# Attention decode with a sliding window: VectorE's and ScalarE's written-out orders become one loop each, and quad 7 gets PSUM banks of its own

## The chip, the cores and the metric

The kernel runs on one core of a Trainium2 chip. The metric is the device time in microseconds (us) of one execution; lower is better. The kernel before took 183.55 us (median of three runs, 183.39 to 183.97).

## The reference

One decoding step of attention with grouped heads over the last W = 512 positions of a cache, with both projections. All data are bf16.

```python
q = (x @ wq).reshape(B, 1, 32, 128).transpose(0, 2, 1, 3)          # B = 32, D = 512
k = repeat(k_cache[:, :, Sk - W:, :], 4, axis=1)                  # 8 heads of keys and values
v = repeat(v_cache[:, :, Sk - W:, :], 4, axis=1)                  # Sk = 2048, Dh = 128
p = softmax(einsum("bhqd,bhkd->bhqk", q, k) * 128 ** -0.5)
out = einsum("bhqk,bhkd->bhqd", p, v).transpose(0, 2, 1, 3).reshape(B, 1, 4096) @ wo
```

The window of the keys is 33.5 MB, that of the values as much, and wq and wo are 4.2 MB each: 75.5 MB are read.

## The kernel before

The 32 sequences are worked on in eight **quads** of four (NQ = 8). A quad q has a load of keys Kq and one of values Vq, 4.2 MB each, and K_sb and V_sb hold two quads each (buffer q % 2). Every step of a quad is an operation with a letter, and every engine has a list of them that is run strictly in order:

- **T**q.w (VectorE, `turn`, L514): the two halves of the keys are turned by 32 x 32 blocks, into KT_sb. It needs Kq, and the scores of the quad before to have read KT_sb.
- **S**q.w (TensorE, `scores`, L340): 16 matmuls for each half give the scores in the PSUM bank S_ps.
- **M** (VectorE): the largest score of a row; **X** (ScalarE): the exponential and its sum; **N** (VectorE): the division, into P_bf.
- **E** (TensorE, `to_value_rows`, L356): 16 matmuls bring the weights to the rows of the values, in EP_ps; **G** (ScalarE) copies them to PTc; **B**q.h (both engines, four heads each) spreads them into bd[q % 2].
- **P**q.a.b (TensorE, `pv`, L368): groups a to b of the 32 groups (four matmuls each) of weights times values, into the four banks O_ps.
- **C**q.r (either engine): a quarter of the rows is picked from O_ps into C_sb; **F** (TensorE, `fold`, L380): eight matmul records that fold it; **D** (ScalarE): the result goes to o_sel.

The orders are text at L19 to L38. TensorE has a head, a loop of three rounds of two quads (L22, L440), and a tail. In a round the quad c is worked on while the values of the quad before it, b, are multiplied; the order is `S{c}.0 S{c}.1 F{a} P{b}.0.12 E{c} P{b}.12.16 P{b}.16.20 P{b}.20.32`, with a the quad before b. For c = 5 this reads S5.0 S5.1 F3 P4.0.12 E5 and the rest of P4. VectorE and ScalarE have a list for all eight quads (L30, L35), without a loop. VectorE's list is not regular: T1.0 stands ahead of M0, T6.0 ahead of M5, T6.1 ahead of N5 and B5, T7.0 ahead of N6 and T7.1 ahead of B6:

```python
T4.1 M4 N4 B4.0.4 T5.0 C3.2.3 T5.1 C3.3.4 T6.0 M5 T6.1 N5 B5.0.4 C4.2.4 M6 T7.0 N6 T7.1 B6.0.4
C5.2.4 M7 N7 B7.0.5 C6.2.4 C7.2.4
```

`needs` (L105) says which operations an operation waits for; one engine's waits for another's are made from it, one semaphore for an engine and a kind of operation.

SyncE issues the large loads in the order of L40: K0 K1 V0 K2 V1 K3 V2 K4 V3 K5 K6 V4 K7 V5 V6 V7 W, where V5, V6 and V7 are two pieces each and W (wo) three. Kq waits for T of quad q - 2, Vq for the P that last read its buffer, and wo, which takes the place of the even keys, for T6.1. The three loads of wo cover rows 0 to 21, 22 to 29 and 30 to 31 of each partition (L46), and the last matmuls (L467) wait for them one after the other.

The eight PSUM banks are S_ps, EP_ps, four for O_ps, F_ps and Y_ps (L180). Since every quad's values go to the same O_ps, Pq waits for all four Cq-1.

Ahead of quad 0, x is turned and multiplied with wq, the eight PSUM banks of queries are copied one at a time (L505, L559), and VectorE turns them (L508).

Of the kernel before, what the change touches and what calls it, by code (L numbers as in the profile page):

```python
# [19 lines left out]
S0.0 S0.1 S1.0 S1.1 E0 E1 P0.0.32  # L20
# [6 lines left out]
P7.0.18 P7.18.32 F6 F7  # L27
"""
ROUNDS = 3
DVE_OPS = """  # L30
T0.0 T0.1 T1.0 M0 T1.1 N0 M1 N1 B0.0.4 B1.0.4 T2.0 T2.1 M2 N2 B2.0.4 T3.0 T3.1 M3 N3 B3.0.4 T4.0
T4.1 M4 N4 B4.0.4 T5.0 C3.2.3 T5.1 C3.3.4 T6.0 M5 T6.1 N5 B5.0.4 C4.2.4 M6 T7.0 N6 T7.1 B6.0.4
C5.2.4 M7 N7 B7.0.5 C6.2.4 C7.2.4
"""
ACT_OPS = """  # L35
X0 X1 G0 B0.4.8 G1 B1.4.8 C0.0.4 X2 D0 G2 B2.4.8 C1.0.4 X3 D1 G3 B3.4.8 C2.0.4 X4 D2 G4 B4.4.8
C3.0.2 X5 D3 G5 B5.4.8 C4.0.2 X6 D4 G6 B6.4.8 C5.0.2 X7 D5 G7 B7.5.8 C6.0.2 C7.0.2 D6 D7
"""  # L38
# [7 lines left out]
WOP = [(0, 22), (22, 30), (30, 32)]  # L46

# [5 lines left out]
def bass_standalone__sliding_block_cached__sampling_kernel(  # L53
# [22 lines left out]
    NG = 4  # L76
# [7 lines left out]
    orders = {"PE": head + sum(rounds, []) + tail, "DVE": ops_of(DVE_OPS), "ACT": ops_of(ACT_OPS)}  # L84

    ends, total = {}, {}
    for eng, ops in orders.items():
        for op in ops:
            kind = op[0]
            key = ("ANY", "C") if kind == "C" else (eng, kind)  # L90
            total[key] = total.get(key, 0) + (op[3] - op[2] if kind == "C" else 1)
            if kind == "C":
                ends["C", op[1]] = key + (4 * op[1] + 4,)
            elif kind == "B":
                for i in range(op[2], op[3]):
                    ends[kind, op[1], i] = key + (total[key],)
            elif kind == "P":
                for g in range(op[2], op[3]):
                    ends["P", op[1], g] = key + (total[key],)
            elif kind == "D":  # L100
                ends[op] = key + (total[key] + 1,)
            else:
                ends[op] = key + (total[key],)

    def needs(op):  # L105
# [3 lines left out]
        if kind == "T":  # L109
            d = [("S", q - 1, op[2])]  # L110
        elif kind == "S":
            d = [("T", q, op[2]), ("X", q - 1)]
        elif kind == "M":
            d = [("S", q, 1)]
        elif kind == "X":
            d = [("M", q), ("N", q - 1)]
        elif kind == "N":
            d = [("X", q), ("E", q - 1)]
        elif kind == "E":
            d = [("N", q), ("G", q - 1)]  # L120
        elif kind == "G":
            d = [("E", q)] + spread(q - NG)
        elif kind == "B":
            d = [("G", q), ("P", q - 2, 31)]
        elif kind == "P":
            d = spread(q) + [("C", q - 1)]
        elif kind == "C":
            d = [("P", q, 31), ("F", q - 2)]
        elif kind == "F":
            d = [("C", q)]  # L130
        elif kind == "D":
            d = [("F", q)]
        return [ends[n] for n in d if n[1] >= 0]

    with ExitStack() as es:
# [3 lines left out]
        K_sb = [sb(f"K_sb{i}", [P, R * DH], BF16) for i in range(2)]  # L139
# [9 lines left out]
        PTc = sb("PTc", [P, NG, R, REP], BF16)  # L149
        C_sb = sb("C_sb", [P, 2, 4, DH], F32)  # L150
        o_sel = sb("o_sel", [P, NI, B], BF16)
# [3 lines left out]
        maxv = sb("maxv", [P, NQ], F32)  # L155
        negmax = sb("negmax", [P, NQ], F32)
        sums = sb("sums", [P, NQ], F32)
        recip = sb("recip", [P, NQ], F32)
# [10 lines left out]
        F_id = spare[:, 1280:1536].bitcast(F32).rearrange("p (r h) -> p r h", r=4)  # L169
        m_id = spare[:, 1536:1792].bitcast(F32).rearrange("p (b h k) -> p b h k", b=4, h=HKV)  # L170
        F_hd = spare[:, 1792:1856].bitcast(F32)
        m_red = spare[:, 1856:1920].bitcast(F32)
# [7 lines left out]
        S_ps, EP_ps, O_ps, F_ps, Y_ps = ps[:, 0], ps[:, 1], ps[:, 2:6], ps[:, 6], ps[:, 7]  # L180

        def folds(q):
            return (F_ps if q < NQ - 1 else S_ps)[:, 0:4 * NI]
# [57 lines left out]
        def _(sp):  # L241
            wait = Waits(sp)
            wo_h = wo.rearrange("(h r) n -> h (r n)", r=DH)
            wo_r = wo_h.rearrange("h (d m) -> h d m", d=4)
            for op in ops_of(" ".join(LOADS)):
                kind, q = op[0], op[1]
                if kind == "K":
                    if q >= 2:
# [13 lines left out]
                else:  # L262
                    wait([ends["T", NQ - 2, 1]])
                    i0, i1 = WOP[q]
                    sp.dma_start(
                        wo_sb[:, i0:i1, :].rearrange("p i n -> p (i n)"),
                        wo_r[:, :, i0 * D:i1 * D],
                    ).then_inc(sem_wo[q], 16)
# [3 lines left out]
        def _(pool):  # L272
# [10 lines left out]
            pool.sem_inc(op_sem["ACT", "D"], 1)  # L283
# [3 lines left out]
            diag(F_id[:, :, :], [[-32, 4], [-1, HQ]], "pool_f")  # L287
            diag(m_id[:, :, :, :], [[-32, 4], [-4, HKV], [-1, KB]], "pool_m")
# [30 lines left out]
        def _(pe):  # L319
# [48 lines left out]
            def pv(q, g0, g1):  # L368
                for g in range(g0, g1):
                    for b in range(4):  # L370
                        pr = slice(32 * b, 32 * b + 32)
                        ins = pe.matmul(  # L372
                            O_ps[:, b, :],
# [6 lines left out]
            def fold(q):  # L380
                for d in range(4):
# [3 lines left out]
                        rhs=C_sb[:, q % 2, :, NI * d:NI * d + NI],  # L385
# [11 lines left out]
            def waits_of(op):  # L397
# [3 lines left out]
                if kind == "S" and op[2] == 0:  # L401
                    yield ("ONE", "pool_qbd"), 4 * (q // 2) + 4
                    if q == 0:
                        yield ("ONE", "dve_q"), 4
                        yield ("ONE", "act_q"), 4
                elif kind == "E" and q == 0:
                    yield ("ONE", "pool_e"), 2
                elif kind == "F" and q < NQ - 1:
# [51 lines left out]
            for j, (i0, i1) in enumerate(WOP):  # L460
                pe.wait_ge(sem_wo[j], 16)
                last = j == len(WOP) - 1
                for cs in ((0, 1), (2, 3)) if last else (range(4),):
                    for i in range(i0, i1):
                        for c in cs:
# [3 lines left out]
                                lhsT=o_sel[:, i, :],  # L469
# [6 lines left out]
        def spread_args(q, h):  # L476
            return bd[:, q % 2, :, h, :], PTc[:, q % NG], mask[:, h:h + 1]

        def pick_args(q, r):
            pr = slice(32 * r, 32 * r + 32)  # L480
            return C_sb[pr, q % 2], O_ps[pr, :, r * DH:(r + 1) * DH]

        @block.vector
        def _(dve):
            wait = Waits(dve)
# [5 lines left out]
            dve.tensor_reduce(  # L491
                F_hd[:, :], F_id[:, :, :].rearrange("p r h -> p h r"), AX.X, ALU.add
            ).then_inc(s["dve_c"], 1)
            dve.wait_ge(s["pool_m"], 2)
            dve.tensor_reduce(
                m_red[:, :].rearrange("p (h k) -> p h k", h=HKV),
                m_id[:, :, :, :].rearrange("p b h k -> p h k b"), AX.X, ALU.add,
            ).then_inc(s["dve_c"], 1)
            dve.wait_ge(s["dve_c"], 2)
            dve.tensor_reduce(  # L500
                mask[:, :], m_red[:, :].rearrange("p (h k) -> p h k", h=HKV), AX.X, ALU.add
            ).then_inc(s["dve_c"], 1)
            for n in range(4):
                dve.wait_ge(s["pe_q"], 2 * n + 1)
                dve.tensor_copy(Q_row[:, 1024 * n:1024 * n + 512], ps[:, 2 * n]).then_inc(s["dve_q"], 1)  # L505
            dve.wait_ge(s["dve_q"], 4)
            dve.wait_ge(s["act_q"], 4)
# [6 lines left out]
            def turn(q, w):  # L514
                dve.wait_ge(sem_k[q % 2], 16 * (q // 2 + 1))
                return dve.transpose(  # L516
                    KT_sb[:, w].bitcast(F32).rearrange("p r c t -> p r (c t)"),
                    K_sb[q % 2][:, :].bitcast(F32).rearrange("p (r w c) -> p r w c", r=R, w=2)[:, :, w],
                )

            def maxes(q):
                dve.tensor_reduce(maxv[:, q:q + 1], S_ps, AX.X, ALU.max).then_inc(s["dve_m"], 1)  # L522
                dve.wait_ge(s["dve_m"], q + 1)
                return dve.tensor_scalar(  # L524
                    negmax[:, q:q + 1], maxv[:, q:q + 1], -SCALE, None, op0=ALU.mult)

            def norm(q):
                dve.reciprocal(recip[:, q:q + 1], sums[:, q:q + 1]).then_inc(s["dve_r"], 1)
                dve.wait_ge(s["dve_r"], q + 1)
                return dve.tensor_scalar(  # L530
                    P_bf[:, :], P_f32[:, :], recip[:, q:q + 1], None, op0=ALU.mult)

            def spread(q, h0, h1):
                for h in range(h0, h1):
                    o, i, m = spread_args(q, h)
                    ins = dve.tensor_scalar(o, i, m, None, op0=ALU.mult)  # L536
                return ins

            def pick(q, r0, r1):
                for r in range(r0, r1):  # L540
                    dve.tensor_copy(*pick_args(q, r)).then_inc(op_sem["ANY", "C"], 1)  # L541

            run = {"T": turn, "M": maxes, "N": norm, "B": spread, "C": pick}
            for op in orders["DVE"]:
                wait(needs(op))
                ins = run[op[0]](*op[1:])
                if ins:
                    ins.then_inc(op_sem["DVE", op[0]], 1)
# [4 lines left out]
        def _(act):  # L553
            wait = Waits(act)
            act.wait_ge(s["pool_j"], 1)
            act.activation(junk[:, 1:2], junk[:, 0:1], ACTF.Exp).then_inc(s["act_warm"], 1)
            for n in range(4):
                act.wait_ge(s["pe_q"], 2 * n + 2)
                act.activation(  # L559
                    Q_row[:, 1024 * n + 512:1024 * n + 1024], ps[:, 2 * n + 1], ACTF.Copy  # L560
                ).then_inc(s["act_q"], 1)
            act.wait_ge(s["dve_c"], 3)

            def exponential(q):
                return act.activation(  # L565
                    P_f32[:, :].rearrange("p (k r) -> p k r", k=KB),
                    S_ps.rearrange("p (r k) -> p k r", k=KB), ACTF.Exp,
                    bias=negmax[:, q:q + 1], scale=SCALE, accum_out=sums[:, q:q + 1],
                )

            def gather(q):
                return act.activation(  # L572
# [57 lines left out]
```

## Time and profile before

| | us |
|---|---|
| median of three runs | 183.55 |
| profiled execution | 183.87 |
| its span (first to last instruction) | 182.6 |
| TensorE matmul busy | 118.9 |
| VectorE busy | 105.8 |
| ScalarE busy | 49.7 |
| mean DMA rate over the span | 415 GB/s |
| mean granted TensorE clock | 0.822 |

In the profile's rows, PE is TensorE (PEld its weight loads), DVE is VectorE, ACT is ScalarE, POOL is GpSimd and SPq is SyncE's queue of DMA issues. A row of the timeline gives its start, its length, the engine, the line of the kernel, the operation, what it writes and reads with the shape, and the count; the bracket gives the idle time of the engine just before it, and what ended that. A row of stages gives for each stretch its length, then each engine's busy time with its count of instructions, then the granted TensorE clock, the share of time in which the DMA engines were busy, and their rate.

### The profile page before, as it was taken

How to read it: one execution, taken by the hardware profiler on the slowest of the kernel's cores; microseconds unless marked ns; L12 is line 12 of the kernel's file. 1: busy time of each engine (PE TensorE's matmuls, PEld its weight loads, DVE VectorE, ACT ScalarE, POOL GpSimd, SP SyncE). 2: the span in 40 equal slices, each digit the busy share in tenths (PEclk: the TensorE clock that was granted, in tenths of full speed). 3: DMA queues.
4: the chain of work that ended last, by engine and by line, in shares of the span. 5: the costliest groups of instructions: out<-in, count | busy, mean ns of one | idle time of the engine just before them, and what ended most of it. 6: DMA issues, size and time to landing. Idle time of an engine off the chain costs nothing.

```text
span 182.6 us, 3659 instructions
## 1 busy us (share of the span) xinstructions
PE 118.9 (65%) x1636; PEld 57.6 (32%) x1636; DVE 105.8 (58%) x101; ACT 49.7 (27%) x92; POOL 12.4 (7%) x34
## 2 busy tenths in 40 slices
PE   0029901425869898049954899334299869996984
PEld 0013300101535353015521453003035434552553
DVE  0031499999559713983279317999902799633030
ACT  3001300000490527402470107100106406443031
POOL 7400012000300000003000000003000000000000
PEclk9999995555769999756995589755559999999999
DMA  6999999999999999999999999999999999999991
GB/s 235 461 431 409 424 459 438 431 395 460 449 431 388 449 456 416 395 452 449 425 398 438 438 447 409 431 438 445 424 416 416 427 424 438 416 436 437 424 374 56
DMA packets 3461, 75.70 MB, mean 415 GB/s; under 512 B 412, under 2 KB 508, under 8 KB 636
## 3 DMA queue, kind: packets, MB, share of 16 engines
q1 hardware_dynamic: 3360, 75.52, 96.7%
q8 instruction: 7, 0.11, 0.3%
q10 hardware_dynamic: 92, 0.05, 0.1%
q14 instruction: 2, 0.02, 0.0%
HBM read 75.53 MB, written 0.03 MB: 414 GB/s over the span
## 4 chain that ended last, share of the span: by engine, by line
DMA 39%; PE 28%; DVE 25%; ACT 3%; issue 3%; SPq 0%; DVEq 0%
DVE KT_sb L516 20%; DMA K_sb<-in_k_cache_dram 16%; DMA V_sb<-in_v_cache_dram 16%; PE ps L372 16%; DMA V_sb<-in_wq_dram 7%; PE ps L334 5%; PE ps L346 3%; DVE QT_sb L508 2%; PE ps L360 2%; ACT bd L578 1%; PE ps L382 1%; DVE C_sb L541 1%; PE ps L467 1%; DVE maxv L522 1%; DVE bd L536 1%
## 5 line engine op out<-in xcount | busy, mean ns | idle before, releaser
L516 DVE STREAM_TRANSPOSE KT_sb<-K_sb 128x4096 f32<-128x4096 f32 x16 | 70.5, 4429 | 4.6 <-DMA K_sb<-in_k_cache_dram 4.5
L372 PE MATMUL ps<-V_sb,bd 32*128 32x512 bf16 x1024 | 62.7, 398 | 9.6 <-DMA V_sb<-in_v_cache_dram 6.5
L346 PE MATMUL ps<-KT_sb,QBD 128*32 128x512 bf16 x256 | 24.6, 527 | 36.2 <-DVE KT_sb L516 32.1
L372 PEld LDWEIGHTS ps<-V_sb,bd 32*128 32x128 bf16 x1024 | 27.0, 97 | 40.5 <-issue 9.8
L346 PEld LDWEIGHTS ps<-KT_sb,QBD 128*32 128x32 bf16 x256 | 6.6, 113 | 52.4 <-DVE KT_sb L516 35.4
L536 DVE TENSOR_SCALAR bd<-PTc,mask 128x512 bf16<-128x512 bf16 x33 | 9.4, 349 | 22.5 <-ACT PTc L572 22.5
L565 ACT ACTIVATE P_f<-ps,negmax 128x512 f32<-128x512 f32 x8 | 5.5, 689 | 58.0 <-DVE negmax L524 58.0
L578 ACT ACTIVATE bd<-PTc,mask 128x512 bf16<-128x512 bf16 x31 | 19.9, 712 | 0.3
L583 ACT ACTIVATE C_sb<-ps 32x512 f32<-32x512 f32 x22 | 13.0, 589 | 21.7 <-PE ps L372 21.4
L541 DVE COPY C_sb<-ps 32x512 f32<-32x512 f32 x10 | 6.9, 693 | 12.9 <-PE ps L372 12.7
L312 POOL COPY QBD<-QT_sb 32x256 bf16<-32x256 bf16 x16 | 6.3, 396 | 106.0 <-PE ps L346 91.2
L572 ACT ACTIVATE PTc<-ps 128x512 bf16<-128x512 f32 x8 | 4.8, 595 | 27.9 <-PE ps L360 27.9
L382 PE MATMUL ps<-C_sb,F_pad 128*128 128x128 f32 x64 | 12.0, 345 | 0.4 <-DVE C_sb L541 0.4
L382 PEld LDWEIGHTS ps<-C_sb,F_pad 128*128 128x128 f32 x64 | 10.2, 242 | 4.8 <-issue 2.9
L360 PE MATMUL ps<-P_bf,E_sb 128*128 128x128 bf16 x128 | 9.5, 233 | 2.2 <-DVE P_bf L530 2.2
L334 PE MATMUL ps<-V_sb,bd 128*128 128x512 bf16 x32 | 9.2, 459 | 1.9 <-DMA V_sb<-in_wq_dram 1.9
L360 PEld LDWEIGHTS ps<-P_bf,E_sb 128*128 128x128 bf16 x128 | 8.1, 105 | 6.3 <-issue 3.4
L522 DVE TENSOR_REDUCE maxv<-ps 128x1 f32<-128x512 f32 x8 | 5.5, 687 | 7.5 <-PE ps L346 7.5
L323 PE MATMUL ps<-bd 32*128 32x128 bf16 x4 | 0.6, 294 | 10.6 <-DMA bd<-in_x_dram 10.6
L487 DVE CAST bd<-ps 128x512 bf16<-128x512 f32 x1 | 0.7, 691 | 11.3 <-PE ps L323 11.3
L559 ACT ACTIVATE KT_sb<-ps 128x512 bf16<-128x512 f32 x4 | 2.4, 598 | 17.1 <-PE ps L334 17.1
L505 DVE CAST KT_sb<-ps 128x512 bf16<-128x512 f32 x4 | 2.8, 692 | 6.7 <-PE ps L334 6.7
(29 smaller groups left out, 31.0 us busy)
## 6 DMA issues: line engine op xcount, KB each, us to landing
K_sb<-in_k_cache_dram SPq DMA_DIRECT2D x8, 4096.0 KB, 24.6
V_sb<-in_v_cache_dram SPq DMA_DIRECT2D x5, 4096.0 KB, 29.4
V_sb<-in_v_cache_dram SPq DMA_DIRECT2D x4, 2048.0 KB, 21.0
V_sb<-in_wq_dram SPq DMA_DIRECT2D x1, 4096.0 KB, 12.3
K_sb<-in_wo_dram SPq DMA_DIRECT2D x1, 2816.0 KB, 20.9
V_sb<-in_v_cache_dram SPq DMA_DIRECT2D x1, 2304.0 KB, 13.1
V_sb<-in_v_cache_dram SPq DMA_DIRECT2D x1, 1792.0 KB, 14.8
K_sb<-in_wo_dram SPq DMA_DIRECT2D x1, 1024.0 KB, 22.7
```

The source lines that it names most:

```text
L312: pool.tensor_copy(QBD[pr].rearrange("p u a (h c) -> p u a h c", h=HKV).rearrange("p u (w t) h c -> p (u w) t h c", w=2)[:, :, :, :, 4 * b ...
L334: ins = pe.matmul(ps[:, n], lhsT=xT_sb[:, kt, :], rhs=wq_sb[:, kt, n * 512:(n + 1) * 512], start=kt == 0, stop=kt == DKT - 1, tile_positio ...
L346: ins = pe.matmul(S_ps[32 * c:32 * c + 32, :], lhsT=QBD[:, q % 2, 2 * w + t, c0:c0 + 32], rhs=KT_sb[:, w, :, KB * h:KB * h + KB, t], start ...
L360: ins = pe.matmul(EP_ps[:, e * R:(e + 1) * R], lhsT=window[:, KB - 1 - k:KB - 1 - k + P], rhs=P_bf[:, k * R:(k + 1) * R], start=k == 0, st ...
L372: ins = pe.matmul(O_ps[:, b, :], lhsT=bd[pr, q % 2, 4 * g:4 * g + 4].rearrange("p r h e -> p (r h e)"), rhs=V_sb[q % 2][pr, 512 * g:512 * ...
L382: ins = pe.matmul(folds(q), lhsT=F_sb[:, d].rearrange("p h d -> p (h d)"), rhs=C_sb[:, q % 2, :, NI * d:NI * d + NI], start=d == 0, stop=d ...
L516: return dve.transpose(KT_sb[:, w].bitcast(F32).rearrange("p r c t -> p r (c t)"), K_sb[q % 2][:, :].bitcast(F32).rearrange("p (r w c) -> ...
L522: dve.tensor_reduce(maxv[:, q:q + 1], S_ps, AX.X, ALU.max).then_inc(s["dve_m"], 1)
L536: ins = dve.tensor_scalar(o, i, m, None, op0=ALU.mult)
L541: dve.tensor_copy(*pick_args(q, r)).then_inc(op_sem["ANY", "C"], 1)
L578: ins = act.activation(o, i, ACTF.Copy, scale=m)
L583: act.activation(*pick_args(q, r), ACTF.Copy).then_inc(op_sem["ANY", "C"], 1)
```

## The change

1. **VectorE and ScalarE run a loop over the eight quads.** Its body is, for quad n, on VectorE: T n.0, T n.1, C of quad n - 2 (its rows 2 and 3), M n, N n, B n (heads 0 to 3). On ScalarE: X n, D of quad n - 2, G n, B n (heads 4 to 7), C of quad n - 1 (rows 0 and 1). What is left of quads 6 and 7 follows the loop. Buffers and semaphore levels are chosen by registers, and the semaphores start from levels that SyncE adds (BIAS), so that the first iterations need no special case. PTc, the maxima and the sums have one buffer in place of four or eight.
2. **Quad 7's values go to PSUM banks 4 to 7**, the other quads' to banks 0 to 3. P7 waits for D5 in place of C6. The folds of quads 6 and 7 go to banks 0 and 1.
3. **The loads of wo** are cut at elements 11264 and 15616 of a partition's 16384, and the last 768 elements (1536 B) come in two loads, of 125 and of 3 partitions.
4. In TensorE's head, E0 stands ahead of S1, and P0 is cut in pieces; P7 is cut in four pieces in place of two. TensorE's loop is unchanged.
5. The copies of the queries are two of 1024 columns on each engine in place of four of 512, and one small reduction is dropped.

The core of the diff:

```diff
 HEAD_OPS = """
-S0.0 S0.1 S1.0 S1.1 E0 E1 P0.0.32
+S0.0 S0.1 E0 S1.0 S1.1 P0.0.12 E1 P0.12.16 P0.16.20 P0.20.32
...
 TAIL_OPS = """
-P7.0.18 P7.18.32 F6 F7
+P7.0.12 P7.12.16 P7.16.18 P7.18.32 F6 F7
...
+WO_LOADS = [(0, 11264), (11264, 15616), (15616, 16384, 125)]
...
+    for n in range(NQ):
+        orders["DVE"] += [("T", n, 0), ("T", n, 1)] + (
+            [("C", n - 2, 2, 4)] if n > 1 else []) + [("M", n), ("N", n), ("B", n, 0, 4)]
+        orders["ACT"] += [("X", n)] + ([("D", n - 2)] if n > 1 else []) + [
+            ("G", n), ("B", n, 4, 8)] + ([("C", n - 1, 0, 2)] if n else [])
+    orders["DVE"] += [("C", LAST - 1, 2, 4), ("C", LAST, 2, 4)]
+    orders["ACT"] += [("C", LAST, 0, 2), ("D", LAST - 1), ("D", LAST)]
+    BIAS = {("PE", "S"): 2, ("PE", "E"): 1, ("PE", "P"): PIECES + 1, ("PE", "F"): 2, ("ACT", "D"): 1}
...
         elif kind == "P":
-            d = spread(q) + [("C", q - 1)]
+            d = spread(q) + [("C", q - 1) if q < LAST else ("D", q - 2)]
...
-        S_ps, EP_ps, O_ps, F_ps, Y_ps = ps[:, 0], ps[:, 1], ps[:, 2:6], ps[:, 6], ps[:, 7]
+        O_ps, S_ps, EP_ps, F_ps, Y_ps = ps[:, 0:4], ps[:, 4], ps[:, 5], ps[:, 6], ps[:, 7]
...
+        def sums_of(b, q):
+            return ps[:, b if q < LAST else 4 + b]
...
+                    c0, c1, *cuts = WO_LOADS[q]
+                    for p0, p1 in zip([0] + cuts, cuts + [P]):
+                        sp.dma_start(
+                            wo_f[p0:p1, c0:c1], wo_p[p0:p1, c0:c1]
+                        ).then_inc(sem_wo[q], 16)
...
+            with dve.Fori(0, NQ) as n:
+                odd = dve.snap(n % 2)
+                one = dve.snap(n + 1)
+                pieces = dve.snap(PIECES * n + 1)
+                landed = dve.snap(16 * (n // 2) + 16)
+                turned = [dve.snap(2 * n + w + 1) for w in range(2)]
...
+                with dve.If(odd):
+                    turn(1)
+                with dve.Else():
+                    turn(0)
+                with dve.If(n > 1):
+                    dve.wait_ge(op_sem["PE", "P"], pieces)
+                    for r in (2, 3):
+                        dve.tensor_copy(*pick_args(r)).then_inc(op_sem["ANY", "C"], 1)
+                dve.wait_ge(op_sem["PE", "S"], 2 * n + 4)
...
+                dve.wait_ge(op_sem["ACT", "G"], one)
+                for h in range(4):
+                    ins = dve.tensor_scalar(
+                        bd[:, bass.ds(odd, 1), :, h, :].rearrange("p o r e -> p (o r) e"),
+                        PTc[:, :, :], mask[:, h:h + 1], None, op0=ALU.mult)
+                ins.then_inc(done("B"), 1)
...
+            with act.Fori(0, NQ) as n:
+                odd = act.snap(n % 2)
+                one = act.snap(n + 1)
+                act.wait_ge(op_sem["DVE", "M"], one)
...
+                with act.If(n > 1):
+                    act.wait_ge(op_sem["PE", "F"], one)
+                    folded(bass.ds(4 * n, 4), 0).then_inc(done("D"), 1)
+                act.wait_ge(op_sem["PE", "E"], n + 2)
...
+                with act.If(n > 0):
+                    act.wait_ge(op_sem["PE", "P"], PIECES * n + PIECES + 1)
+                    for r in (0, 1):
+                        act.activation(*pick_args(r), ACTF.Copy).then_inc(op_sem["ANY", "C"], 1)
```

## Prediction

> **What bounds the kernel now.** I read the page's slices first: is anything busy throughout?
>
> ```profile
> DMA  6999999999999999999999999999999999999991
> q1 hardware_dynamic: 3360, 75.52, 96.7%
> q8 instruction: 7, 0.11, 0.3%
> ```
>
> The load stream is: 75.5 MB at 415 GB/s, without a hole from the second slice to the last but one. The kernel ends when the stream ends, as long as no engine falls behind it. The next question is how far behind VectorE may fall. The timeline around quad 4, then around quads 5 to 7 (VectorE, TensorE and ScalarE rows), tells it:
>
> ```profile
> 92.28 8.77 DVE L516 STREAM_TRANSPOSE KT_sb<-K_sb 128x4096 f32<-128x4096 f32 x2 [1.18 <-DMA K_sb<-in_k_cache_dram]
> 101.11 1.90 PE L346 MATMUL ps<-KT_sb,QBD 128*32 128x512 bf16 x16 [2.35 <-DVE KT_sb L516]
> 102.94 2.08 PE L382 MATMUL ps<-C_sb,F_pad 128*128 128x128 f32 x8
> 104.95 3.40 PE L372 MATMUL ps<-V_sb,bd 32*128 32x512 bf16 x48
> 108.28 1.07 PE L360 MATMUL ps<-P_bf,E_sb 128*128 128x128 bf16 x16
> 110.02 1.14 DVE L536 TENSOR_SCALAR bd<-PTc,mask 128x512 bf16<-128x512 bf16 x4 [4.55 <-ACT PTc L572]
> ...
> 122.12 4.45 DVE L516 STREAM_TRANSPOSE KT_sb<-K_sb 128x4096 f32<-128x4096 f32 x1
> ...
> 127.39 4.43 DVE L516 STREAM_TRANSPOSE KT_sb<-K_sb 128x4096 f32<-128x4096 f32 x1
> ...
> 131.15 5.31 PE L372 MATMUL ps<-V_sb,bd 32*128 32x512 bf16 x48 [5.83 <-DMA V_sb<-in_v_cache_dram]
> 136.39 1.34 PE L360 MATMUL ps<-P_bf,E_sb 128*128 128x128 bf16 x16
> 138.40 1.14 DVE L536 TENSOR_SCALAR bd<-PTc,mask 128x512 bf16<-128x512 bf16 x4 [6.00 <-ACT PTc L572]
> 142.08 1.91 PE L346 MATMUL ps<-KT_sb,QBD 128*32 128x512 bf16 x32
> ```
>
> Quad 4's rows are one whole chain T, S, F, P.0.12, E, G, B: from 92.28 to 111.16, 18.88 us. The same chain took 18.46 for quad 3 (72.65 to 91.11) and 16.46 for quad 2 (53.38 to 69.84). Two loads take 19.4 (K4 landed at 92.28, K5 at 111.72), so the chain just fits, with VectorE idle for only 1.18. The second group shows how quads 5 to 7 fit: P4.0.12 waits until 131.15 for V4, E5 and B5 stand behind it, and VectorE uses that wait to turn quad 6's keys (122.12 and 127.39), ahead of B5. So S6 runs at 142.08 in one piece, and T7 ends at 154.20.
>
> **The change, step by step.**
>
> *The loop's order (the term that decides).* In the loop T n+1 stands behind B n, always. TensorE's order and the loads' order are unchanged, so E5 still stands behind P4.0.12, and that behind V4. T6 thus moves from 122 to after B5, and T7 to after B6. Queued behind the waiting B5 on VectorE: T6, so S6, so P5 on TensorE, so everything to the end. Two whole chains that had been overlapped come after 131.15.
>
> First, whether VectorE reaches that point in time. The last copy of the queries begins at 22.40 as before and reads two banks: between 0.60 (as now) and 1.20 (double); I take 1.0, so T0 starts 0.4 later, at 27.15. T0 8.77, S0.1 1.90 (the row at 35.58), M to X 0.91, X to N 1.01, N 0.49, E0 1.71 (its row at 46.86), G 0.60, B 1.14, with gaps: B0 ends at 43.85. T1 follows (before: 35.45, ahead of B0); 8.77, S1.1 1.90, P0.0.12 3.40 (quad 3's row); E1 starts at 57.95. From E's start to B's end took 2.88 in quad 2 (66.96 to 69.84), so B1 ends at 60.85. Then a chain each for quads 2, 3 and 4, at 18.7 (the mean of quads 3 and 4, since TensorE will stand idle before each half of S, as there): T3 at 79.6, T4 at 98.3, T5 at 117.0; their keys landed at 72.65, 92.28 and 111.72, earlier. T5 ends at 125.8, and 3.9 later (as in quad 4: 101.06 to 104.95) P4.0.12 could start: 129.7. V4 comes at 131.15. The head's delay of some 8 us is eaten up by then; 1.45 is left.
>
> Do the loads stay without a hole? K6 is issued when T4 ends, at 107.1 (before: 101.08), while the stream has work until K5 lands, 111.72: a lead of 4.6. V7's first piece, behind the first 20 groups of P5, comes to 155.6 (before: 152.86), with V6 landing near 160.4 (131.15 plus three loads of 9.75): a lead of 4.8. The store of 16 KB at the end takes 1.4 from issue to landing, so 4.6 should do.
>
> Now the end. P4.0.12 from 131.15 follows closely on S5 and F3, so I take quad 2's 2.99 rather than 5.31: E5 at 134.07, B5's end at 136.95.
> - T6 to B6: 18.7. B6 ends at 155.7.
> - T7 to B7: 18.7. B7 ends at 174.4.
> - From E's start to the end of P's last group took 5.51 in quad 6 (160.96 to 166.47), so P6 ends 5.51 - 2.88 = 2.63 after B7: 177.0.
> - P7, 128 matmuls: 7.09, to 184.1.
> - C7, F7, D7, the last projection, the store: 175.27 to 182.6 before, 7.33.
>
> The span is then 191.45. The profiled execution had 1.27 outside its span, which gives 192.7, and it lay 0.32 above the median of the runs: **192.4 us**.
>
> *Quad 7's own banks.* This line is what it removes:
>
> ```profile
> 168.18 7.09 PE L372 MATMUL ps<-V_sb,bd 32*128 32x512 bf16 x128 [1.72 <-DVE C_sb L541]
> ```
>
> P7 no longer waits for C6: 1.72 less. It is in the sum already (P7 directly behind P6). Quad 7's keys are late next, not its values, which landed before 172 in this profile.
>
> *The loads of wo.* Rows of the stages at the end (us, busy times with counts, clock, DMA share, GB/s):
>
> ```profile
> 178.00:179.00 1.00, 0.69 (x51) 0.69 (x54) 0.00 (x0) 0.26 (x1) 0.00 (x0) 1.00 0.42 166
> 179.00:180.00 1.00, 1.00 (x84) 0.99 (x72) 0.00 (x0) 0.00 (x0) 0.00 (x0) 1.00 0.18 55
> ```
>
> The last two us move bytes at a share of 0.42 and 0.18: some DMA engines end later than others. Whatever the new cut does there, wo lands near 180 and is needed at 187; the cover is 7 us, so nothing. Without it: from 0.6 saved (0.42 and 0.18 of an us are all that runs there) to 1.8 lost (one issue more, 0.43, and a small transfer by itself, 1.4 as the store's).
>
> *At nothing.* C n-2 on VectorE behind T n: 1.42 beside S's 1.90 (if S takes 1.05, 0.4 shows in each quad). One PTc, one bank set for the maxima: each next writer stands behind the last reader on the chain anyway. ScalarE's C and D: it is idle there (27% busy). P7 in four pieces: the values are there. The dropped reduction runs during the wait for wq.
>
> *The loops' own cost.* No row shows a loop on VectorE. The nearest is TensorE's: at 142.08 its third round begins directly behind P4's last matmul, so the turn costs nothing. On VectorE the turn is issued while B's 1.14 run, which should hide it: I take 0. The other end is 1.4 a turn (the store's issue to landing, if instructions had to be fetched). With o a turn, five turns come before P4.0.12 (cover 1.45) and two after: the end moves by max(0, 5o - 1.45) + 2o, 8.35 for 1.4.
> By the Trainium skill's Runtime: NRT & Kernel Launch, Instruction fetch mechanics, a taken branch whose target is outside the two pages of instructions held stalls on a fetch. TensorE's loop was fetched with 7 packets in all (q8 above), with no stall at its turn, so the trace doesn't show it.
>
> **Rivals.**
> 1. *TensorE stays fast* in quads 6 and 7, and both chains take quad 2's 16.46: 4.5 less, 187.9. For it: P4's rest runs until 139.6, 1.8 before S6.0. Against: between S6.0 and S6.1 it idles for 3.3 again, and in quad 4 a gap of 2.35 left the granted clock at 0.50. The Trainium skill's TensorE: Matmul & The Clock Gate, What's actually happening, has the clock halved after an idle window of about 3.4 us; by it alone the gaps here are on the edge.
> 2. *Turns that cost*, or K6 with too small a lead (o over 0.8 turns its 4.6 into the store's 1.4): 195.5 to 200.8, by the formula for o from 0.65 to 1.4.
> 3. *Faster:* the stream still sets the end, and P7's 1.72 are gained: 181.8. It decides at D7: to start it at 177.98 or earlier, T7 must start by 177.98 - 2.71 - 7.09 - 2.63 - 18.7 = 146.85, so T6 by 128.1. That needs P4.0.12 some 9 us ahead of V4's landing. Against it speaks every row above; for it, that the stream is all the page shows as full.
> 4. *No difference:* the engines run otherwise than the loop's text says. Nothing speaks for it.
>
> **Chances.** Forecast (189.5 to 195.5) 0.77; rival 1 0.08; rival 2 0.10; rival 3 0.03; rival 4 0.02. A measurement of this kernel tells about 0.3% from no change; faster by more 0.03, within 0.02, slower by more 0.95. The range, 188 to 198, takes in rival 1 and rival 2 up to o = 1.0, and leaves out some 0.1.
>
> **What would show it.** In the changed profile: T6 starts within 0.3 of B5's end, near 137, and T7 near 155.7; idle time of VectorE ahead of its B's, not ahead of its T's; the DMA slices fall before the end, with wo landed 7 us before its matmuls; P7 directly behind P6. Wrong if a T6 row stands ahead of B5's, if DMA's nines go on to the last slice, if VectorE idles by over 0.5 between B and T, or if S6 and S7 run at 1.05 a half.

## The result and the profile after

The changed kernel takes 194.96 us (median of four runs, 194.22 to 196.56); the kernel before took 183.59 in the same comparison. The ratio is 1.063 (95% interval 1.055 to 1.070): slower by 11.4 us. In all that follows a ratio leaves out the runs that lie over 1.5% above their kernel's fastest; a median takes in all. The profiled execution of the changed kernel took 195.54, with a span of 194.1.

The page of the changed kernel, the same three lines as of before:

```profile
DMA  6999999999999999999999599999999999999300
q1 hardware_dynamic: 3352, 75.52, 91.3%
q8 instruction: 7, 0.11, 0.2%
```

The nines end three slices (some 15 us) ahead of the end, and there is a hole in slice 23. The stream no longer sets the end. T0, and the chain of quads 5 to 7, in the timeline (rows of VectorE and TensorE; those left out are marked by three dots):

```profile
28.61 8.77 DVE L511 STREAM_TRANSPOSE KT_sb<-K_sb 128x4096 f32<-128x4096 f32 x2 [0.72 <-DVE QT_sb L491]
...
129.27 1.90 PE L338 MATMUL ps<-KT_sb,QBD 128*32 128x512 bf16 x16 [3.28 <-DVE KT_sb L511]
131.10 2.08 PE L374 MATMUL ps<-C_sb,F_pad 128*128 128x128 f32 x8
...
133.45 3.55 PE L364 MATMUL ps<-V_sb,bd 32*128 32x512 bf16 x48 [0.28 <-DMA V_sb<-in_v_cache_dram]
136.93 1.07 PE L352 MATMUL ps<-P_bf,E_sb 128*128 128x128 bf16 x16
...
138.79 1.14 DVE L540 TENSOR_SCALAR bd<-PTc,mask 128x512 bf16 x4 [5.09 <-ACT PTc L583]
140.06 8.77 DVE L511 STREAM_TRANSPOSE KT_sb<-K_sb 128x4096 f32<-128x4096 f32 x2
...
157.03 1.14 DVE L540 TENSOR_SCALAR bd<-PTc,mask 128x512 bf16 x4 [3.71 <-ACT PTc L583]
158.18 8.77 DVE L511 STREAM_TRANSPOSE KT_sb<-K_sb 128x4096 f32<-128x4096 f32 x2
...
175.40 11.40 PE L364 MATMUL ps<-V_sb,bd 32*128 32x512 bf16 x208
176.25 1.14 DVE L540 TENSOR_SCALAR bd<-PTc,mask 128x512 bf16 x4 [4.82 <-ACT PTc L583]
```

T6 follows B5 by 0.13, T7 follows B6 by 0.01: VectorE's idle time stands ahead of its B's, where it waits for E and G, and never ahead of a T for keys. P7 runs directly behind P6 (208 matmuls in one row). F3 ended at 133.18, and P4.0.12 waited only another 0.28 for V4: by then the chain itself had come nearly as late as V4.

The hole, from the stages of the changed kernel (the last two columns are the DMA share and GB/s):

```profile
108.00:110.00 2.00, 0.00 (x0) 0.00 (x0) 2.00 (x1) 0.00 (x0) 0.00 (x0) 0.50 0.65 279
110.00:112.00 2.00, 1.02 (x12) 0.45 (x16) 1.94 (x3) 0.00 (x0) 0.00 (x0) 0.50 0.00 0
```

K6 was issued when T4 ended, at 110.9, and by then the stream had been dry for about a microsecond.

### The profile page after: what moved, and what is told of

Its sections match the earlier page's. It is cut to its first block, busy times and chain, and to the rows that moved or that the text cites. A ratio compares the mean times of both kernels' runs of the same rounds, so it can differ in the third digit from the quotient of the medians.

```text
span 194.1 us, 3854 instructions
## 1 busy us (share of the span) xinstructions
PE 123.0 (63%) x1636; PEld 58.9 (30%) x1636; DVE 109.8 (57%) x103; ACT 46.9 (24%) x85; POOL 12.6 (6%) x34
## 4 chain that ended last, share of the span: by engine, by line
PE 37%; DVE 21%; DMA 18%; issue 18%; ACT 3%; DVEq 2%; SPq 0%; ACTq 0%
PE ps L364 17%; DVE KT_sb L511 16%; DMA V_sb<-in_v_cache_dram 11%; DMA V_sb<-in_wq_dram 6%; PE ps L338 6%; PE ps L326 5%; PE ps L374 5%; PE ps L352 4%; ACT PTc L583 2%; DVE QT_sb L491 2%; DVE bd L540 1%; PE ps L459 1%; DVE C_sb L547 1%; ACT KT_sb L557 1%; DVEq L508 0%
## 5 line engine op out<-in xcount | busy, mean ns | idle before, releaser
L338 PE MATMUL ps<-KT_sb,QBD 128*32 128x512 bf16 x256 | 26.1, 547 | 52.5 <-DVE KT_sb L511 52.5
L364 PEld LDWEIGHTS ps<-V_sb,bd 32*128 32x128 bf16 x1024 | 26.1, 97 | 32.6 <-issue 7.6
L540 DVE TENSOR_SCALAR bd<-PTc,mask 128x512 bf16 x32 | 9.1, 350 | 33.1 <-ACT PTc L583 33.1
L588 ACT ACTIVATE bd<-PTc,mask 128x512 bf16 x32 | 20.5, 710 | 1.4 <-ACT PTc L583 1.4
L374 PE MATMUL ps<-C_sb,F_pad 128*128 128x128 f32 x64 | 14.4, 396 | 0.4 <-DVE C_sb L547 0.4
L374 PEld LDWEIGHTS ps<-C_sb,F_pad 128*128 128x128 f32 x64 | 12.5, 291 | 6.1 <-DVE C_sb L524 5.0
L326 PE MATMUL ps<-V_sb,bd 128*128 128x512 bf16 x32 | 9.9, 486 | 1.9 <-DMA V_sb<-in_wq_dram 1.9
L595 ACT ACTIVATE C_sb<-ps 32x512 f32<-32x512 f32 x14 | 8.2, 587 | 7.9 <-PE ps L364 7.7
L524 DVE COPY C_sb<-ps 32x512 f32<-32x512 f32 x12 | 8.3, 693 | 0.4
L547 DVE COPY C_sb<-ps 32x512 f32<-32x512 f32 x4 | 2.8, 693 | 8.1 <-PE ps L364 8.0
L315 PE MATMUL ps<-bd 32*128 32x128 bf16 x4 | 0.6, 295 | 10.7 <-DMA bd<-in_x_dram 10.7
L486 DVE CAST KT_sb<-ps 128x1024 bf16<-128x1024 f32 x2 | 2.4, 1224 | 7.8 <-PE ps L326 7.8
## 6 DMA issues: line engine op xcount, KB each, us to landing
K_sb<-in_wo_dram SPq DMA_DIRECT2D x1, 2816.0 KB, 18.1
V_sb<-in_v_cache_dram SPq DMA_DIRECT2D x1, 2304.0 KB, 10.3
```

The source lines that it names most:

```text
L326: ins = pe.matmul(ps[:, n], lhsT=xT_sb[:, kt, :], rhs=wq_sb[:, kt, n * 512:(n + 1) * 512], start=kt == 0, stop=kt == DKT - 1, tile_positio ...
L338: ins = pe.matmul(S_ps[32 * c:32 * c + 32, :], lhsT=QBD[:, q % 2, 2 * w + t, c0:c0 + 32], rhs=KT_sb[:, w, :, KB * h:KB * h + KB, t], start ...
L364: ins = pe.matmul(sums_of(b, q), lhsT=bd[pr, q % 2, 4 * g:4 * g + 4].rearrange("p r h e -> p (r h e)"), rhs=V_sb[q % 2][pr, 512 * g:512 * ...
L374: ins = pe.matmul(folds(q), lhsT=F_sb[:, d].rearrange("p h d -> p (h d)"), rhs=C_sb[:, q // LAST, :, NI * d:NI * d + NI], start=d == 0, st ...
L524: dve.tensor_copy(*pick_args(r)).then_inc(op_sem["ANY", "C"], 1)
L540: ins = dve.tensor_scalar(bd[:, bass.ds(odd, 1), :, h, :].rearrange("p o r e -> p (o r) e"), PTc[:, :, :], mask[:, h:h + 1], None, op0=ALU ...
```

## The experiments

The theory was that the loop's order makes one chain T, S, F, P.0.12, E, G, B of all quads, of which the last two turns stand behind V4. The rivals were the loops' own cost, the wait for V4 with the hole in the stream, and the new loads of wo.

**The order alone** (`order_only`), the kernel before with VectorE's and ScalarE's lists in the loop's order, and TensorE's head to suit:

```diff
-T0.0 T0.1 T1.0 M0 T1.1 N0 M1 N1 B0.0.4 B1.0.4 T2.0 T2.1 M2 ...
+T0.0 T0.1 M0 N0 B0.0.4 T1.0 T1.1 M1 N1 B1.0.4 T2.0 T2.1 C0.2.4 M2 N2 B2.0.4 T3.0 T3.1 C1.2.4 M3 ...
...
-S0.0 S0.1 S1.0 S1.1 E0 E1 P0.0.32
+S0.0 S0.1 E0 S1.0 S1.1 P0.0.12 E1 P0.12.32
...
```

> The kernel before, with the two lists put into the order of the loop's body (and TensorE's head as the change has it, which that order needs); no loop, no new banks, no new loads. Theory 'order' (T behind B makes one chain of VectorE, TensorE and ScalarE over all quads): the 194.96 of the changed kernel, less what its loops seem to cost in its trace (0.72 ahead of the first T, 0.12 between G and B in 8 quads, 0.14 ahead of every second T: 2.2 in all), less some 0.8 of the later copies of the queries, plus 1.7 since P7 waits for C6 again: 193.7, between 191.5 and 195.5. Rival 'loops': the order costs little by itself, 184 to 187. T6 stands behind B5 in both.

It took 193.47, ratio 1.053 (1.050 to 1.056). The order by itself costs 10.0 us, so rival 'loops', by which it costs little, fails. P7 still waits for C6 in this kernel:

```profile
178.75 7.09 PE L369 MATMUL ps<-V_sb,bd 32*128 32x512 bf16 x128 [1.72 <-DVE C_sb L538]
```

**The loops written out** (`loops_unrolled`), the changed kernel with constants in place of registers:

```diff
-            with dve.Fori(0, NQ) as n:
+            for n in range(NQ):
...
-                        bd[:, bass.ds(odd, 1), :, h, :].rearrange("p o r e -> p (o r) e"),
+                        bd[:, odd:odd + 1, :, h, :].rearrange("p o r e -> p (o r) e"),
...
```

> The changed kernel with VectorE's and ScalarE's loops written out eight times with constants, all else as it is. Theory 'order': only the loops' own 2.2 go, 192.7 (191.5 to 194), and the gap between G and B goes back from 0.15 to 0.03. Rival 'loops': 184 to 187.

It took 191.19 (190.71 to 193.99), ratio 1.041 (1.040 to 1.043): 3.8 less than with the loops (194.22 to 196.56), more than the 2.2 that I had counted in gaps. Here V4 is what P4.0.12 waits for, and the rest of the sum can be read off its timeline:

```profile
131.03 2.77 PE L364 MATMUL ps<-V_sb,bd 32*128 32x512 bf16 x48 [1.88 <-DMA V_sb<-in_v_cache_dram]
...
135.46 1.14 DVE L537 TENSOR_SCALAR bd<-PTc,mask 128x512 bf16<-128x512 bf16 x4 [5.76 <-ACT PTc L580]
136.52 8.77 DVE L511 STREAM_TRANSPOSE KT_sb<-K_sb 128x4096 f32<-128x4096 f32 x2
...
154.79 8.77 DVE L511 STREAM_TRANSPOSE KT_sb<-K_sb 128x4096 f32<-128x4096 f32 x2
...
171.48 1.14 DVE L537 TENSOR_SCALAR bd<-PTc,mask 128x512 bf16<-128x512 bf16 x4 [3.44 <-ACT PTc L580]
```

B5 ends at 136.60, T7 starts at 154.79, B7 ends at 172.62: the predicted chain, with 18.3 and 17.8 for a quad in place of 18.7.

**VectorE's loop alone written out** (`dve_unrolled`, the same diff in VectorE's block only):

> The changed kernel with VectorE's loop alone written out; ScalarE's stays. Writing out both took 3.8 off. If VectorE's branches and register operations (ahead of the first T, ahead of every second T, between G and B) are the cost: 191 to 192.5. If ScalarE's share (its wait for E by a register) is as large: 193 to 194.

It took 193.00 with a spread of 190.74 to 194.85, ratio 1.046 (1.041 to 1.050). The median lies at the lower edge of the second expectation, the ratio (some 192.0) in the first, and the spread covers both: how the 3.8 are shared between the engines stays open.

**The late and the early part of the order.** First the late part alone (`late_order`):

```diff
-T6.0 M5 T6.1 N5 B5.0.4 C4.2.4 M6 T7.0 N6 T7.1 B6.0.4 C5.2.4 M7 N7 B7.0.5 C6.2.4 C7.2.4
+M5 N5 B5.0.4 C4.2.4 T6.0 T6.1 M6 N6 B6.0.4 C5.2.4 T7.0 T7.1 M7 N7 B7.0.5 C6.2.4 C7.2.4
```

> The kernel before with only the late part of VectorE's list put in order: T6 behind B5 and T7 behind B6; quads 0 to 5 as they were. Theory 'the late overtaking is all': V4 lands at 131.15 and sets the clock anew, TensorE is slow then as before (5.31), B5 ends at 139.5, two chains of 18 to 18.7 follow, and P7 waits for C6 again: 193 to 196. Rival 'the delay is gathered over all quads': the two late chains lose only their own share of it, 186 to 189.

It took 204.47, ratio 1.115 (1.111 to 1.120), 8.5 more than the theory's upper end. The list was not the one I meant: C4 and C5 stand ahead of T6 and T7, so each T also waits for the whole of P4 or P5. In its trace T6 starts at 142.53, behind a C4 that TensorE released at 141.08, where B5 had ended at 138.41. With the C's behind the T's, as the loop has them (`late_order_2`):

```diff
-T6.0 M5 T6.1 N5 B5.0.4 C4.2.4 M6 T7.0 N6 T7.1 B6.0.4 C5.2.4 M7 N7 B7.0.5 C6.2.4 C7.2.4
+M5 N5 B5.0.4 T6.0 T6.1 C4.2.4 M6 N6 B6.0.4 T7.0 T7.1 C5.2.4 M7 N7 B7.0.5 C6.2.4 C7.2.4
```

> The kernel before with T6 directly behind B5 and T7 directly behind B6, and C4 and C5 behind T6 and T7 as the loop has them (the first try put them ahead, so that each T waited for all of P4 and P5 as well). Theory 'the late overtaking is all': B5 ends near 138.5, two chains of 18 to 18.7, 2.63 to P6's end, 1.7 of P7's wait for C6, 7.09 and 7.33: a span of 193.5 to 195, 194.7 to 196.3. Rival: the first try's 204.5 came from something else in the late part, and 200 or more stay.

196.20, ratio 1.067 (1.064 to 1.069): inside the theory's interval. The late part costs 2.7 more than the whole order did. 1.1 of it is there when B5 ends: VectorE gets to quad 5 early, TensorE stands still for 5.86 before V4 comes, and P4.0.12 then takes 5.31 (4.30 in `order_only`).

The early part alone (`early_order`):

```diff
-T0.0 T0.1 T1.0 M0 T1.1 N0 M1 N1 B0.0.4 B1.0.4
+T0.0 T0.1 M0 N0 B0.0.4 T1.0 T1.1 M1 N1 B1.0.4
-X0 X1 G0 B0.4.8 G1 B1.4.8
+X0 G0 B0.4.8 X1 G1 B1.4.8
```

> The kernel before with only the early part in order: M0, N0 and B0 ahead of T1 (with TensorE's head and ScalarE's first steps to suit); T6 and T7 overtake as they did. Theory 'the late overtaking is all': K3 is issued 8 later and T2 starts 7 later, but P4.0.12 still waits for V4, and the time stays 183.5 to 184.1. Rival 'gathered over all quads': 186 to 190.

184.46, ratio 1.005 (1.003 to 1.006): 1.0 slower, a little over the theory's 0.6. T5 starts at 116.95 in place of 111.72, and that is nearly all gone at V4: E5 starts at 137.68 in place of 136.39. So the loss comes from T6 and T7, as the sum had it. The two parts (12.6 and 1.0) do not add up to the 10.0 of the whole order; why was not tried.

**E ahead of P.0.12** (`e_first`), the changed kernel with TensorE's order altered for every quad, in the head and in the loop:

```diff
...
-S{c}.0 S{c}.1 F{a} P{b}.0.12 E{c} P{b}.12.16 P{b}.16.20 P{b}.20.32
+S{c}.0 S{c}.1 F{a} E{c} P{b}.0.12 P{b}.12.16 P{b}.16.20 P{b}.20.32
```

> The changed kernel with E ahead of P.0.12 of the quad before in TensorE's head and loop; nothing else. Theory 'one chain from T to B': P.0.12 (2.8 to 3.9 in a quad) leaves the chain, a quad takes 16 to 16.5 in place of 18 to 19.6, E5 no longer stands behind V4, and the load stream sets the end again: 183.5 to 187. Rival 'registers and branches, or VectorE's own work, are too slow': P.0.12 was beside other waits, and 192 or more stay.

184.28, ratio 1.005 (1.003 to 1.006): with the loops, their registers and VectorE's regular order all in place, 10.7 of the 11.4 us are gone. VectorE, quads 4 and 5 and T7 of this kernel:

```profile
106.19 0.49 DVE L535 TENSOR_SCALAR P_bf<-P_f,recip 128x512 bf16<-128x512 f32 x1
108.58 1.14 DVE L540 TENSOR_SCALAR bd<-PTc,mask 128x512 bf16 x4 [1.91 <-ACT PTc L583]
111.70 8.77 DVE L511 STREAM_TRANSPOSE KT_sb<-K_sb 128x4096 f32<-128x4096 f32 x2 [1.98 <-DMA K_sb<-in_k_cache_dram]
...
147.90 8.77 DVE L511 STREAM_TRANSPOSE KT_sb<-K_sb 128x4096 f32<-128x4096 f32 x2
```

B4 follows N4 by 1.9 in place of the 3.7 to 5.1 of quads 1 to 7 in the changed kernel, and VectorE waits for keys again (1.98 before T5). T7 starts 10.3 earlier than in the changed kernel (158.18).

**V4 loaded ahead of K6** (`v4_first`), in the changed kernel:

```diff
-K0 K1 V0.0 K2 V1.0 K3 V2.0 K4 V3.0 K5 K6 V4.0 K7 V5.0 ...
+K0 K1 V0.0 K2 V1.0 K3 V2.0 K4 V3.0 K5 V4.0 K6 K7 V5.0 ...
```

> The changed kernel with V4 loaded ahead of K6. V4 lands some 10 earlier and the stream has no hole before it. Theory 'one chain': TensorE waited only 0.28 for V4 in the changed kernel, so 194 to 195.5, no difference. Rival 'V4 and the hole in the stream': 191 to 192.5, as the prediction's sum would have it where V4 sets B5.

194.28 (193.10 to 195.25), ratio 1.058 (1.053 to 1.063): no difference clear of the spread. The hole is filled, as its stages show,

```profile
108.00:110.00 2.00, 0.08 (x4) 0.09 (x8) 1.97 (x2) 0.00 (x0) 0.00 (x0) 0.50 1.18 508
110.00:112.00 2.00, 2.00 (x17) 0.62 (x18) 1.41 (x3) 0.00 (x0) 0.00 (x0) 0.50 0.99 426
```

and nothing clear of the spread comes of it: the medians differ by 0.7. Neither the hole nor V4 is what costs the 11.4 us.

**Quad 7's banks alone** (`banks_only`), in the kernel before:

```diff
-            d = spread(q) + [("C", q - 1)]
+            d = spread(q) + [("C", q - 1) if q < LAST else ("D", q - 2)]
...
-                            O_ps[:, b, :],
+                            sums_of(b, q),
...
```

> The kernel before with quad 7's own PSUM banks alone. P7 starts 1.7 earlier. Theory: the last load of wo landed at about 180.1 there, just ahead of its matmuls at 180.23, so the stream takes over at once and 0.1 to 0.4 are gained: 183.3. Rival: the wait was the last thing in the way, and 1.5 are gained: 182.1.

183.56, ratio 1.000 (0.999 to 1.001): nothing. TensorE's last rows show who took the place of the wait that went:

```profile
176.96 1.41 PE L471 MATMUL ps<-K_sb,o_sel 128*32 128x128 bf16 x88 [0.91 <-DMA K_sb<-in_wo_dram]
179.35 0.91 PE L471 MATMUL ps<-K_sb,o_sel 128*32 128x128 bf16 x40 [0.99 <-DMA K_sb<-in_wo_dram]
```

D7 is over at 176.36 (178.26 before), and then each load of wo is waited for in turn. In the changed kernel the stream is long over by then, and the wait of 1.72 that `order_only` still has ahead of P7 is not there; that the edit saves the whole 1.7 there was not tried by itself.

**The loads of wo alone** (`wo_only`), in the kernel before:

```diff
+WO_LOADS = [(0, 11264), (11264, 15616), (15616, 16384, 125)]
...
```

> The kernel before with the new cut of the loads of wo alone. Theory: D7 and the 2.05 of matmuls behind it set the end, wo lands earlier unseen: 183.6, within 0.3%. Rival: the load of 125 partitions runs on few DMA engines, lands later than before and adds 0.5 to 1.5: 184.1 to 185.1.

184.33, ratio 1.004 (1.003 to 1.006): the rival was right, 0.8 slower. TensorE's last matmuls, which follow D7 at once for the first load, wait for the other two:

```profile
178.00 1.41 PE L468 MATMUL ps<-K_sb,o_sel 128*32 128x128 bf16 x88 [0.37 <-ACT o_sel L587]
179.84 0.63 PE L468 MATMUL ps<-K_sb,o_sel 128*32 128x128 bf16 x32 [0.43 <-DMA K_sb<-in_wo_dram]
180.72 0.30 PE L468 MATMUL ps<-K_sb,o_sel 128*32 128x128 bf16 x8 [0.25 <-DMA K_sb<-in_wo_dram]
```

The last eight end at 181.02, 0.7 later than before (178.31 plus 2.05, 180.36). In the Trainium skill, DMA: Bandwidth & Descriptors, Why a DMA increments its semaphore by 16 and not by 1, a load runs on the largest number of DMA engines up to 16 that divides its count of partitions; an estimate by that rule is 5 for 125. The late landing agrees with it; on how many engines the load ran, no row here shows.

**E first, with the old loads of wo**, with the loops (`e_first_old_wo`) and with both written out (`e_first_unrolled`):

```diff
-WO_LOADS = [(0, 11264), (11264, 15616), (15616, 16384, 125)]
+WO_LOADS = [(0, 11264), (11264, 15360), (15360, 16384)]
```

> The changed kernel with E ahead of P.0.12 and the loads of wo as before (22, 8 and 2 rows). Theory: with the short chain the stream sets the end, and the new cut's 0.8 is what stands between 184.28 and the kernel before: 183.3 to 183.8. Rival: the rest is the loops' own cost, and 184.2 stays.

> The same with both loops written out. If the stream sets the end, the loops' 3.8 us are hidden behind it and nothing changes against the kernel with the loops: 183.2 to 183.7, no difference from the kernel before either. Rival: VectorE's chain still counts, and 182 or less come out.

They took 186.17 (184.25 to 186.44), ratio 1.012 (1.009 to 1.016), and 184.95 (184.20 to 186.51), ratio 1.009 (1.006 to 1.013). Both theories miss, and by the medians so do their rivals. The fastest runs of all three kernels with E first agree (184.23, 184.25, 184.20), which speaks against the loops and wo as what is left. The trace of `e_first` points to a new chain, TensorE's own; no run tries it by itself:

```profile
131.04 9.42 PE L364 MATMUL ps<-V_sb,bd 32*128 32x512 bf16 x128 [4.13 <-DMA V_sb<-in_v_cache_dram]
140.39 1.91 PE L338 MATMUL ps<-KT_sb,QBD 128*32 128x512 bf16 x32
```

All of P4 now stands between V4 and S6, and from there D7 starts at 178.40, with the stream ending at about the same time. Why many runs of the last two take 186 and none of the four of `e_first` does was not found. No kernel of these beats the one before.

## Why the prediction was right, and where its sizes were off

*The loop's order decides:* right, and shown. The order alone costs 10.0; without P.0.12 in the chain 10.7 of the 11.4 go.

*Two whole chains come after V4:* right for the kernel with the loops written out (B5 predicted to end at 136.95, measured 136.60), and the late part of the order by itself costs more than the loss. In the changed kernel itself the step "1.45 is left" did not hold: T5 started at 120.44 in place of 117.0, F3 ended at 133.18 in place of 129.7, and V4 only 0.28 later. There the whole row of turns decides, and not V4's landing (`v4_first`). To end with the stream, T7 would have to start by 146.85 (the prediction's rival 3), which from the predicted T0 at 27.15 is an estimated 17.1 a turn. The changed kernel's seven turns from T0 to T7 (28.61 to 158.18) took 18.5 each, those of `e_first` (27.23 to 147.90) 17.2.

*The loops' own cost:* this is the term that was mis-sized. It was put down as 0, hidden behind B, with 8.35 as the other end; writing the loops out measured 3.8. Its visible parts are not the turn itself, which costs 0 to 0.14: the first T starts 0.72 behind the transpose of the queries, and B starts 0.15 behind G in place of 0.03 in every quad. In that gap VectorE has only the wait for G, and the writes into `bd` go to a buffer that a register chooses; what fills the 0.12 no row shows. These gaps add up to some 2.2. The other 1.6 of the 3.8 need not be the loops': the last copy of the queries, ahead of both loops, began at 23.15 in the profiled execution of the changed kernel, at 21.80 in that of the unrolled one, and at 21.76 in `e_first`, which has the loops. By the prediction's own formula 3.8 is o = 0.75, in what rival 2 covered, but no turn in the rows costs that much. No more instructions were fetched with the loops either: all kernels have the seven packets of q8, and the page of the kernel before has two more, on a queue q14, that the changed kernel's page does not have.

*The loads stay without a hole:* wrong, with no effect clear of the spread. K6 came at 110.9 in place of 107.1, and the stream, taken to last until K5's landing at 111.72, was running out between 109 and 110.

*18.7 for a chain:* 19.5, 18.1 and 19.2 for quads 5, 6 and 7, so the slow TensorE clock was the right choice against rival 1. The stage from 108 to 112, between the halves of S4, has the clock at 0.50. The gaps were not on the edge: in the kernel before the clock fell from 1.00 to 0.50 near 96.0, 2.3 after the matmuls that ended at 93.72, and in the changed kernel near 107.8, right behind a half of S that followed a gap of 2.21. One sign of being wrong came half true: S6 took 1.29 and 1.90, S7 1.05 and 1.90, so one half of S7 ran at the fast figure.

*Quad 7's banks:* right that P7 follows P6 and no longer waits for C6. Rival 3's way of gaining the 1.72 at the end of the stream failed also in the kernel before (`banks_only`). *The loads of wo:* right for this kernel, and in the kernel before inside the given bound of 1.8 lost.

*The head:* T0 came at 28.61 in place of 27.15: 0.75 since the last copy of the queries began at 23.15 and not 22.40, behind TensorE, and 0.7 at the loop's entry. The copy of two banks took 1.02, as chosen.

In all the span was 194.1 in place of 191.45, and the median of the runs 194.96 in place of 192.4. That it came so near is in part luck: misses of opposite sign partly cancel. With the loops written out the kernel takes 191.19, 1.2 below the forecast, and with the loops, put down at nothing, 2.6 above it.

## What to carry to other kernels

An irregular order in a list is worth reading as a schedule: look for the wait that each displaced step filled, and for what bounds the stage then. Before such a list is rolled into a loop, take the longest dependency through one turn (here T, S, F, P.0.12, E, G, B) and compare it with the time that one turn may take. That is not the time of the turn's own loads: two loads took 19.4 here, and turns of 18.5 still made the kernel slower, since the first turn starts some 27 us into the stream and some 17 us of work stand behind the end of the last; the estimated bound was 17.1. The step to move is the one that stands on that chain without feeding it (P.0.12), on whichever engine it is. An edit that removes a wait is to be tried in the state in which it will run: the same banks were worth nothing ahead of a full stream, while behind an empty one (`order_only`) the wait that they remove is 1.72 on the path.

## What the runs showed of the hardware

- Loops of eight turns on VectorE and on ScalarE: 194.96 with them, 191.19 written out, in runs that spread by 1.2% and 1.7%. A turn showed a gap of at most 0.14, the entry 0.72, and each start of B behind G 0.12 more.
- Writing the orders out took two more instruction packets (q14, 2) than the loops did (none); one loop of the two written out took one (`dve_unrolled`).
- The kernel that the stream sets is steady (183.39 to 183.97), the kernels that the chain sets spread by 0.8% (`order_only`) to 2.2% (`dve_unrolled`). In the changed kernel's trace the same 48 matmuls took 2.77 us where the granted clock was 1.00 (at 114.74 and 152.47), and 3.55 and 3.62 where it was 0.54 and 0.50 for their first 1.75 us (at 133.45 and 170.85), and that is on the path. That this makes the spread of the runs is likely but not shown, with one trace of each kernel.
- Cutting the last 196 KB of a full stream into loads of 125 and 3 partitions made the last matmuls end 0.7 later, and the time 0.8 longer.
